# Transposes ahead of the value product in an attention and gated-convolution kernel

## The chip, the cores and the metric

The kernel runs on one core of one Trainium2 chip. The metric is the device time of one execution in microseconds (us); the figure for a kernel is the median of several executions. A core has five engines that run side by side, each with its own queue of instructions: TensorE (PE in the profile; its weight loads have a row of their own, PEld), VectorE (DVE), ScalarE (ACT), GpSimd (POOL) and SyncE (SP), which here only issues DMAs. TensorE writes its results to PSUM, a memory of eight banks, from which ScalarE or VectorE must copy them before the bank can be used again.

## The reference

Attention in which a query sees only the keys that fall into its own hash bucket, then a gated convolution and two products with weights. There are 4 batches, 8 heads, 768 positions and 64 numbers per head.

```python
q_bits = (np.einsum('bhsd,dk->bhsk', q, proj) > 0)      # 6 bits; k_bits alike
mask = q_bucket[:, :, :, None] == k_bucket[:, :, None, :]
scores = scale * np.matmul(q, k.transpose(0, 1, 3, 2))
scores = np.where(mask, scores, -1000000000.0)
attn = softmax(scores)
x = np.matmul(attn, v)              # heads side by side: 4 x 768 x 512
gate = sigmoid(causal depthwise convolution of x, 5 taps)
out = (gate * (x @ w_val)) @ w_out
```

## The kernel before, in words

A unit is one head of one batch (32 units), and a tile is 128 queries of a unit (6 per unit, 192 in all). The main loop goes over slots `k`, one per tile, and every engine but SyncE takes its instructions in the order in which the code issues them: the order in the loop's body is the order of the work. The tiles are in a pipeline, so that a slot works on several of them:

- `scores(k + 1)` (L236): TensorE makes the scores of 128 queries against 768 keys, in four products that add up two parts of the numbers, into one of two PSUM buffers `s`. The buffer comes free when `exponentials(k - 1)` has read it.
- `maxima(k)`, `factors(k)`, `shifts(k)` (L242, L248, L252): VectorE finds the rows' maxima and makes the factor `gs` and the shift `nb`.
- `exponentials(k)` (L260): ScalarE makes the exponentials `p` of a tile from `s`, `gs` and `nb`.
- `row_sums`, `recip` (L266, L270), once per two tiles: VectorE; `normalise(k - 2)` (L275): GpSimd multiplies `p` by the reciprocal.
- `transposes(k - 3)` (L284): TensorE transposes the six 128 x 128 blocks of `p`, three into each of two PSUM buffers `tp`. A `tp` buffer comes free when ScalarE has copied it.
- `keep_transposed(k - 4)` (L293), first in a slot: ScalarE copies the two `tp` into `pt`.
- `attn_v` (L307, L315): when the six tiles of a unit are in `pt`, TensorE multiplies them by the values into the PSUM buffer `av`, in six steps (`kb`). `step(avs)` is called twice in each odd slot, so that a unit's product takes three odd slots. Behind the last step, in the same call, ScalarE copies `av` to `x` in two instructions.

Into the same slots come steps of other work: `step(convs)` (the convolution, L327 to L342, mostly VectorE and GpSimd), `step(weights[...])` (the weights' split, in the first 60 slots), `step(moes)` (the two feed-forward products of an earlier batch, L369 and L394: four products of TensorE in a step, from slot 60 or so on, with some slots left out) and `step(preps)` (the next unit's operands: GpSimd's L166 and L169, DMAs, and once in four units `bits`, L197 and L200: TensorE multiplies four units by the hash planes, half in one slot and half in the next, and VectorE makes `u` of them. These products go into a `tp` buffer once a batch's feed-forward work exists, and into a PSUM buffer of their own before that).

Behind the loop stand the last unit's value product and the last batch's feed-forward work.

Of the kernel before, what the change touches and what calls it, by code (L numbers as in the profile page):

```python
# [26 lines left out]
def kernel(  # L27
# [18 lines left out]
    LAG = 3  # L46
# [71 lines left out]
    def load_conv():  # L118
        if conv_w.dtype == mybir.dt.int64:
            w = const.tile([P, NP * KW, 2], I32, name="cw64")  # L120
            nc.sync.dma_start(out=w, in_=conv_w.bitcast(I32).rearrange("p (n t) -> p n t", t=2))
            t = const.tile([P, NP * KW], FP32, name="cwt")
            yield
            a, d = yield from from_float64(w, t)
            yield
            nc.vector.tensor_tensor(out=cw_sb, in0=d, in1=a, op=ALU.add)
        else:
            nc.sync.dma_start(out=cw_sb, in_=conv_w)

    def load_weights(which):  # L130
        parts = [(src[:, c, :], hl[0][:, c, :], hl[1][:, c, :])
                 for src, hl in ((w_val, wv), (w_out, wo)) for c in range(NP)]
        for src, hi, lo in parts[which::2]:
            if src.dtype == mybir.dt.int64:
                w = wst.tile([P, 512, 2], I32, name="w64")
                nc.sync.dma_start(out=w, in_=src.bitcast(I32).rearrange("p (n t) -> p n t", t=2))
            else:
                w = wst.tile([P, 512], FP32, name="w32")
                nc.sync.dma_start(out=w, in_=src)
            yield  # L140
            yield from split_weight(w, hi, lo)

    def load_raw(i):
        if i < len(units):
            b, h = units[i]
            raws[i] = raw.tile([P, S], FP32, name="r")
            nc.sync.dma_start(out=raws[i], in_=qk[b, h])

    def load_values(i):
        b, h = units[i]  # L150
        if h % 2 == 0:
            vts[i] = vp.tile([P, KB, P], FP32, name="vt")
            nc.sync.dma_start(out=vts[i], in_=v[b, h // 2])
        else:
            vts[i] = vts[i - 1]

    def prep(i):

        if i >= len(units):
            return  # L160
        b, h = units[i]
        j = h % 4
        load_values(i)
        r = raws[i]
        aq, ak, bq, bk = stacks[i] = [stk.tile([P, S], FP32R, name=nm) for nm in ("aq", "ak", "bq", "bk")]
        nc.gpsimd.tensor_copy(out=aq, in_=r)  # L166
        if i > 1:
            yield
        nc.gpsimd.tensor_tensor(out=bq, in0=r, in1=aq.bitcast(FP32), op=ALU.subtract)  # L169
        nc.sync.dma_start(out=ak[0:D].bitcast(FP32), in_=aq[D:P].bitcast(FP32))  # L170
        nc.sync.dma_start(out=bk[0:D].bitcast(FP32), in_=aq[D:P].bitcast(FP32))
        nc.sync.dma_start(out=bk[D:P].bitcast(FP32), in_=bq[D:P].bitcast(FP32))
        nc.sync.dma_start(out=bq[D:P].bitcast(FP32), in_=aq[0:D].bitcast(FP32))
        if i == 1:
            yield
        u = cur["u"]
        nc.sync.dma_start(out=aq[D:M].bitcast(FP32), in_=u[32 * j:32 * j + 2 * NB].bitcast(FP32))
        nc.sync.dma_start(out=ak[D:M].bitcast(FP32), in_=u[32 * j + 2 * NB:32 * j + 4 * NB].bitcast(FP32))
        load_raw(i + 5)
        if j == 3 and i + 1 < len(units):  # L180
            yield
            yield from bits(i + 1)
# [21 lines left out]
    def first_bits():  # L204
        yield from bits(0)
        load_raw(5)

    def first_prep():

        r = raws[0]  # L210
        aq, ak, bq, bk = stacks[0] = [stk.tile([P, S], FP32R, name=nm) for nm in ("aq", "ak", "bq", "bk")]
        z = ps_t.tile([P, 512], FP32, name="tp")
        for g in range(4):
            nc.tensor.matmul(out=z[32 * g:32 * g + 2 * NB, 0:HS], lhsT=proj_sb[:, 2 * NB * (g // 2):2 * NB * (g // 2 + 1)],
                             rhs=r[:, HS * (g % 2):HS * (g % 2 + 1)], start=True, stop=True, tile_position=(0, 32 * g))
        nc.scalar.copy(out=aq[0:D], in_=r[0:D])
        nc.vector.tensor_copy(out=bk[D:P], in_=r[D:P])
        nc.vector.tensor_copy(out=ak[0:D], in_=r[D:P])
        nc.gpsimd.tensor_tensor(out=bk[0:D], in0=r[D:P], in1=bk[D:P].bitcast(FP32), op=ALU.subtract)
        for g in (0, 2, 3, 1):  # L220
            if g == 1:
                nc.vector.tensor_tensor(out=bq[D:P], in0=r[0:D], in1=aq[0:D].bitcast(FP32), op=ALU.subtract)  # L222
            nc.vector.tensor_scalar(out=(aq, ak)[g // 2][D:M, HS * (g % 2):HS * (g % 2 + 1)],
                                    in0=z[32 * g:32 * g + 2 * NB, 0:HS],
                                    scalar1=rows_sb[32 * g:32 * g + 2 * NB, 2:3],
                                    scalar2=rows_sb[32 * g:32 * g + 2 * NB, 3:4], op0=ALU.is_ge, op1=ALU.mult)
        nc.scalar.copy(out=bq[0:D], in_=r[0:D])

    def scores(k):
        i, qt = tiles[k]  # L230
        aq, ak, bq, bk = stacks[i]
        qs = slice(qt * P, (qt + 1) * P)
        s = ss[k] = ps_s.tile([P, 2, 512], FP32, name="s")
        for lq, rk, n in ((aq, ak, M), (bq, bk, P)):
            for hf in range(2):
                nc.tensor.matmul(out=s[:, hf, 0:HS], lhsT=lq[0:n, qs],  # L236
                                 rhs=rk[0:n, hf * HS:(hf + 1) * HS], start=n == M, stop=n == P)
# [35 lines left out]
    def normalise(k):  # L273
        p, _ = ps[k]
        nc.gpsimd.tensor_scalar(out=p, in0=p, scalar1=rcs.pop(k), scalar2=1.0, op0=ALU.mult, op1=ALU.mult)  # L275

    def transposes(k):
        p, _ = ps.pop(k)
        tps[k] = []
        for a in range(2):  # L280
            tp = ps_t.tile([P, 512], FP32, name="tp")
            for n in range(3):
                kb = 3 * a + n
                nc.tensor.transpose(out=tp[:, n * P:(n + 1) * P], in_=p[:, kb * P:(kb + 1) * P], identity=ident)  # L284
            tps[k].append(tp)
# [146 lines left out]
    def step(gens):  # L432

        while gens:
            try:
                return next(gens[0])
            except StopIteration:
                gens.pop(0)
# [6 lines left out]
    N = len(tiles)  # L445
    with tc.manual_schedule(engines=ENGINES):
        for i in range(5):
            load_raw(i)
        load_values(0)
        first_prep()  # L450
        weights = [[load_conv(), load_weights(0)], [load_weights(1)]]
        preps = [first_bits(), prep(1)]
        scores(0)
        next(preps[1])
        step(preps)
        step(weights[0])
        step(weights[1])
        turn = 0
        for k in range(N + LAG + 1):
            if 0 <= k - LAG - 1:  # L460
                keep_transposed(k - LAG - 1)
            pair = k % 2 == 0 and 0 <= k - 2 < N
            if k < N:
                maxima(k)
            if pair:
                row_sums(k - 2)
            if k < N:
                factors(k)
            if pair:
                recip(k - 2)  # L470
            if 0 <= k - 2 < N:
                normalise(k - 2)
            if k < N:
                shifts(k)
            if k + 1 < N:
                if tiles[k + 1][0] != tiles[k][0]:
                    finish(preps)
                    preps = [prep(tiles[k + 1][0] + 1)]
                scores(k + 1)
            if k < N:  # L480
                exponentials(k)
            if k >= 60 or k % 2:
                step(convs)
            for _ in range((1, 0, 2, 0, 2, 2)[k % 6]):
                step(weights[turn])
                turn = 1 - turn
            for _ in range(3 if cur["gates"] else 1):
                step(moes)
            cur["gates"] = max(0, cur["gates"] - 1)
            step(preps)  # L490
            if k % 2:
                step(avs)
                step(avs)
            if 0 <= k - LAG < N:
                transposes(k - LAG)
        accs[:] = [(ps_m, "m"), (ps_t, "tp"), (ps_s, "s"), (ps_t, "tp"), (ps_s, "s")]
        finish(avs)
        cur["gates"] = 0
        cur["end"] = True
        while convs:  # L500
            step(convs)
            step(moes)
        finish(moes)
# [59 lines left out]
```

## Time and profile before

| | |
|---|---|
| median of 3 executions | 626.68 us (626.09 to 627.2) |
| profiled execution, its own time | 627.79 us |
| its span, first to last instruction | 625.6 us |
| mean granted TensorE clock | 0.992 |
| TensorE, TensorE's weight loads busy | 588.2 us, 423.0 us |
| VectorE, ScalarE, GpSimd busy | 443.6, 421.3, 396.8 us |

How to read the rows: in a timeline a row has the start and the length in us, the engine, the line of the code, the operation, what it writes and reads, the shape, and how many instructions were merged (x8); in brackets stands how long the engine was idle before it and whose work ended that. A row of the waits has who waited for whom, the total in us, how often, and the longest. TensorE's products of full 32-bit numbers run in two passes, so four products of `attn_v` are eight records. The lengths of TensorE's records overlap: what a group costs is read from its start to the next group's start.

### The profile page before, as it was taken

To read this page: it belongs to the slowest core of one execution; us is meant where nothing else is said; L and a number is where in the kernel's file an instruction comes from. 1 tells how busy PE (TensorE), PEld (TensorE's weight loads), DVE (VectorE), ACT (ScalarE), POOL (GpSimd) and SP (SyncE) were. 2 spreads that over 40 slices of the span, in tenths; PEclk is the share of its full clock that TensorE was granted. 3 is DMA by queue.
4 is the path that set the end of the run, shared out by engine and by line. 5 is a ranking of instruction groups with operands and counts; after the bars stand their busy time and mean duration, and the time that the engine had idled before them with its cause. 6 is when DMAs were issued, how large, how long until landed. Compare 5 with 4: busy or idle time off the path is not lost.

```text
span 625.6 us, 10595 instructions
## 1 busy us (share of the span) xinstructions
PE 588.2 (94%) x3496; PEld 423.0 (68%) x3496; DVE 443.6 (71%) x1017; ACT 421.3 (67%) x881; POOL 396.8 (63%) x373
## 2 busy tenths in 40 slices
PE   5799888889999999999999999999999999999997
PEld 2656555556567777776667777676667777776895
DVE  5979897999876857477666867559575877665532
ACT  3777867677787766677796767667787767665400
POOL 3576978698956766566655768377563777544321
PEclk9799999999999999999999999999999999999999
DMA  6453625343523343224424233343423223300111
GB/s 226 129 156 76 176 70 168 77 122 82 132 72 87 81 124 71 72 81 114 107 78 123 68 79 92 77 113 79 124 56 76 53 46 91 77 18 1 50 51 50
DMA packets 23269, 56.76 MB, mean 91 GB/s; under 512 B 4296, under 2 KB 4296, under 8 KB 23216
## 3 DMA queue, kind: packets, MB, share of 16 engines
q1 hardware_dynamic: 23072, 56.06, 33.7%
q8 instruction: 28, 0.46, 0.3%
q14 instruction: 25, 0.20, 0.1%
q10 hardware_dynamic: 144, 0.03, 0.0%
HBM read 23.12 MB, written 6.29 MB: 47 GB/s over the span
## 4 chain that ended last, share of the span: by engine, by line
PE 66%; DVE 15%; ACT 12%; DMA 3%; issue 2%; POOL 1%; SPq 0%; ACTq 0%; DVEq 0%; POOLq 0%
PE av L307 17%; PE s L236 15%; PE tp L284 12%; PE m L394 8%; PE m L369 7%; ACT p L260 5%; DVE nm L242 5%; ACT pt L293 3%; DVE g L338 3%; ACT x L315 2%; PE tp L369 1%; PE tp L394 1%; PE s L394 1%; DVE u L200 1%; PE s L369 1%
## 5 line engine op out<-in xcount | busy, mean ns | idle before, releaser
L275 POOL TENSOR_SCALAR p<-p,ri 128x768 f32<-128x768 f32 x192 | 212.0, 1108 | 160.1 <-DVE nb L252 141.7
L242 DVE TENSOR_REDUCE nm<-s 128x1 f32<-128x768 f32 x192 | 182.5, 951 | 62.6 <-PE s L236 62.1
L293 ACT COPY pt<-tp 128x384 f32<-128x384 f32 x384 | 166.1, 485 | 85.0 <-PE tp L284 84.1
L260 ACT ACTIVATE p<-s,nb,gs 128x768 f32<-128x768 f32 x192 | 192.6, 1003 | 41.1 <-DVE nb L252 39.5
L284 PEld LDWEIGHTS tp<-ident,p 128*128 128x128 f32 x1152 | 130.1, 141 | 73.9 <-issue 44.7
L284 PE MATMUL tp<-ident,p 128*128 128x128 f32 x1152 | 164.9, 279 | 4.6 <-ACT pt L293 1.8
L307 PE MATMUL av<-pt,vt 128*64 128x384 f32 x768 | 146.2, 502 | 0.0
L236 PE MATMUL s<-ak,aq 76*128 76x384 f32 x384 | 117.8, 388 | 23.6 <-ACT p L260 21.2
L236 PE MATMUL s<-bk,bq 128*128 128x384 f32 x384 | 101.3, 345 | 0.4 <-DVE bq L222 0.4
L307 PEld LDWEIGHTS av<-pt,vt 128*64 128x64 f32 x768 | 47.3, 137 | 63.3 <-issue 62.7
L236 PEld LDWEIGHTS s<-ak,aq 76*128 76x128 f32 x384 | 59.0, 193 | 40.4 <-ACT p L260 36.6
L338 DVE SCALAR_TENSOR_TENSOR g<-x,cw_sb,g 128x768 f32<-128x768 f32 x64 | 83.2, 1300 | 2.2 <-POOL g L336 2.1
L236 PEld LDWEIGHTS s<-bk,bq 128*128 128x128 f32 x384 | 71.4, 193 | 0.8 <-issue 0.8
L380 POOL TENSOR_TENSOR hl<-ht,hh 128x384 fp32r<-128x384 f32 x32 | 32.3, 1009 | 43.7 <-DVE hh L378 43.7
L169 POOL TENSOR_TENSOR bq<-r,aq 128x768 fp32r<-128x768 f32 x31 | 59.1, 1908 | 0.1
L315 ACT COPY x<-av 64x384 f32<-64x384 f32 x64 | 30.4, 475 | 32.5 <-PE av L307 31.9
L252 DVE TENSOR_SCALAR nb<-nm,gs 128x1 f32<-128x1 f32 x192 | 40.5, 211 | 3.5
L369 PE MATMUL m<-xh,wv 128*128 128x384 f32 x200 | 42.7, 337 | 0.0
L374 DVE TENSOR_TENSOR ht<-m,g 128x384 f32<-128x384 f32 x25 | 13.9, 556 | 37.1 <-PE m L369 32.5
L328 POOL TENSOR_TENSOR xl<-x,xh 128x384 fp32r<-128x384 f32 x32 | 33.3, 1056 | 9.8 <-DVE xh L327 9.8
L260 ACT ACTIVATION_READ_ACCUMULATOR p<-s,nb,gs 128x1 f32 x192 | 39.1, 204 | 0.0
L394 PE MATMUL m<-wo,hh 128*128 128x512 f32 x144 | 38.2, 395 | 0.0
(84 smaller groups left out, 488.2 us busy)
## 6 DMA issues: line engine op xcount, KB each, us to landing
r<-in_qk_dram SPq DMA_DIRECT2D x32, 384.0 KB
vt<-in_v_dram SPq DMA_DIRECT2D x16, 384.0 KB
out_dram<-o SPq DMA_DIRECT2D x24, 256.0 KB
ak<-aq SPq DMA_DIRECT2D x31, 192.0 KB
bk<-aq SPq DMA_DIRECT2D x31, 192.0 KB
bk<-bq SPq DMA_DIRECT2D x31, 192.0 KB
bq<-aq SPq DMA_DIRECT2D x31, 192.0 KB
w<-in_w_val_dram SPq DMA_DIRECT2D x4, 512.0 KB
```

Of the source, the lines that this page charges most:

```text
L169: nc.gpsimd.tensor_tensor(out=bq, in0=r, in1=aq.bitcast(FP32), op=ALU.subtract)
L236: nc.tensor.matmul(out=s[:, hf, 0:HS], lhsT=lq[0:n, qs], rhs=rk[0:n, hf * HS:(hf + 1) * HS], start=n == M, stop=n == P)
L242: nc.vector.tensor_reduce(out=nm, in_=s[:, :, 0:HS], axis=AX.XY, op=ALU.max, negate=True)
L260: nc.scalar.activation(out=p, in_=s[:, :, 0:HS], func=AF.Exp, bias=nb, scale=gs.pop(k), accum_out=sm[:, k % 2, 0:1])
L275: nc.gpsimd.tensor_scalar(out=p, in0=p, scalar1=rcs.pop(k), scalar2=1.0, op0=ALU.mult, op1=ALU.mult)
L284: nc.tensor.transpose(out=tp[:, n * P:(n + 1) * P], in_=p[:, kb * P:(kb + 1) * P], identity=ident)
L293: nc.scalar.copy(out=pt[:, :, qo:qo + P], in_=tp[:, 0:HS].rearrange("p (a b) -> p a b", b=P))
L307: nc.tensor.matmul(out=av[s * D:(s + 1) * D, 0:HS], lhsT=vt[:, kb, hh * D:(hh + 1) * D], rhs=pt[kb // 3][:, kb % 3, :], start=(kb == 0), s ...
L315: nc.scalar.copy(out=x[hh * D:(hh + 1) * D, o:o + HS], in_=av[s * D:(s + 1) * D, 0:HS])
L338: nc.vector.scalar_tensor_tensor(out=g, in0=x[:, k:k + S], scalar=w, in1=g, op0=ALU.mult, op1=ALU.add)
L369: nc.tensor.matmul(out=acc[:, 0:HS], lhsT=wv[wi][:, c, j * P:(j + 1) * P], rhs=xs_[(c, o)][xi], start=(m == 0), stop=(m == 11))
L394: nc.tensor.matmul(out=acc, lhsT=hs[(o, j)][hi][:, tb * P:(tb + 1) * P], rhs=wo[wi][:, j, :], start=(m == 0), stop=(m == 11))
```

## The change

In a slot, `transposes(k - 3)` is issued ahead of the two `step(avs)` instead of behind them. Everything else stays. Even slots have no `step(avs)`, so that nothing moves in them.

```diff
             step(preps)
+            if 0 <= k - LAG < N:
+                transposes(k - LAG)
             if k % 2:
                 step(avs)
                 step(avs)
-            if 0 <= k - LAG < N:
-                transposes(k - LAG)
```

On TensorE, an odd slot and the even slot behind it, in a stretch without feed-forward products, before (`s` are scores, `av` the value product, `tp` the transposes):

```order
L236 MATMUL s<-ak,aq 128x384 x2
L236 MATMUL s<-bk,bq 128x384 x2
L307 MATMUL av<-pt,vt 64x384 x4
L284 MATMUL tp<-ident,p 128x128 x6
L236 MATMUL s<-ak,aq 128x384 x2
L236 MATMUL s<-bk,bq 128x384 x2
L284 MATMUL tp<-ident,p 128x128 x6
```

and after:

```order
L236 MATMUL s<-ak,aq 128x384 x2
L236 MATMUL s<-bk,bq 128x384 x2
L284 MATMUL tp<-ident,p 128x128 x6
L307 MATMUL av<-pt,vt 64x384 x4
L236 MATMUL s<-ak,aq 128x384 x2
L236 MATMUL s<-bk,bq 128x384 x2
L284 MATMUL tp<-ident,p 128x128 x6
```

The six transposes of the odd slot now stand next to its scores, and the value product next to the even slot's scores.

On ScalarE the order of the instructions is the same as before. At the end of a unit's value product, in the slot behind the odd one, one wait differs (`x` are the copies of the value product, `pt` those of the transposes, `p` the exponentials; the difference has before as - and after as +):

```order
 L315 COPY x<-av 64x384 [waits PE_49]
 L315 COPY x<-av 64x384
-L293 COPY pt<-tp 128x3x128 [waits PE_49] x2
+L293 COPY pt<-tp 128x3x128 x2
 L260 ACTIVATE p,sm<-s,nb,gs 128x768 [waits DVE_49,Pool_49]
```

The `pt` copies need no wait for TensorE of their own any more: the `x` copies ahead of them wait for an instruction of TensorE that now stands behind the transposes.

VectorE and GpSimd keep their order. SyncE's queue, which is not written out by hand, has three DMAs in another order at some places, as here (`vt` are values, `r` the queries and keys of a later unit, `bq` an operand of the next one):

```order
 L177 DMA aq<-u 12x768
-L153 DMA vt<-in_v_dram 128x768
-L173 DMA bq<-aq 64x768
-L147 DMA r<-in_qk_dram 128x768
+L147 DMA r<-in_qk_dram 128x768
+L153 DMA vt<-in_v_dram 128x768
+L173 DMA bq<-aq 64x768
```

The load of `r` moved ahead of the load of `vt` and of a copy within the core.

## The prediction

> **What bounds the kernel now.** First the page's engine shares, then the waits, then two stretches of the timeline.
>
> ```profile
> PE 588.2 (94%) x3496; PEld 423.0 (68%) x3496; DVE 443.6 (71%) x1017; ACT 421.3 (67%) x881; POOL 396.8 (63%) x373
> ```
>
> TensorE (PE) is busy nearly throughout. So only two things can move the time: the order's own cost on TensorE, and where TensorE waits. From the waits:
>
> ```profile
> ACT x L315 <- PE av L307: 31.9, 30, 3.8
> PEld s L236 <- ACT p L260: 36.6, 54, 2.6
> ```
>
> ScalarE (ACT) waits for the value product before it copies it out (us, times, longest); and 54 times the score product (S) waits for an exponential that must free its PSUM buffer. The timeline shows how these hang together, in a stretch without feed-forward products (start, length, engine). I write A for a slot's value products, T for its transposes; an odd slot is S, A, T, an even one S, T.
>
> ```profile
> 300.02 1.51 PE L307 MATMUL av<-pt,vt 128*64 128x384 f32 x8
> ...
> 301.57 0.97 ACT L315 COPY x<-av 64x384 f32<-64x384 f32 x2 [0.74 <-PE av L307]
> ...
> 302.57 0.86 ACT L293 COPY pt<-tp 128x384 f32<-128x384 f32 x2
> ...
> 303.32 1.01 ACT L260 ACTIVATE p<-s,nb,gs 128x768 f32<-128x768 f32 x1
> ...
> 304.47 0.62 PE L236 MATMUL s<-ak,aq 76*128 76x384 f32 x2 [0.43 <-ACT p L260]
> ...
> 305.38 1.51 PE L307 MATMUL av<-pt,vt 128*64 128x384 f32 x8
> ...
> 306.70 0.19 DVE L252 TENSOR_SCALAR nb<-nm,gs 128x1 f32<-128x1 f32 x1
> ...
> 306.98 0.91 POOL L275 TENSOR_SCALAR p<-p,ri 128x768 f32<-128x768 f32 x1 [1.34 <-DVE nb L252]
> 307.40 0.86 ACT L293 COPY pt<-tp 128x384 f32<-128x384 f32 x2 [1.25 <-PE tp L284]
> ...
> 307.45 0.59 PE L236 MATMUL s<-ak,aq 76*128 76x384 f32 x2
> ...
> 308.15 1.01 ACT L260 ACTIVATE p<-s,nb,gs 128x768 f32<-128x768 f32 x1
> 308.24 0.82 PE L284 MATMUL tp<-ident,p 128*128 128x128 f32 x6
> ...
> 309.30 0.62 PE L236 MATMUL s<-ak,aq 76*128 76x384 f32 x2 [0.24 <-ACT p L260]
> ...
> 314.13 0.62 PE L236 MATMUL s<-ak,aq 76*128 76x384 f32 x2 [0.25 <-ACT p L260]
> ```
>
> Two kinds of slot pairs (an odd slot and the even one behind it) are here. In the first, A is the last third of a head's value product: ScalarE copies x, then pt, then makes the exponential, and S starts. From A's start to that S it takes 304.47 - 300.02 = 4.45 us. I call these x pairs; there is one per head. In plain pairs x is absent; from 309.30 to 314.13 such a pair lasts 4.83 us, and the S behind its T (308.24 to 309.30, 1.06 us) still waits for an exponential. ScalarE does not overtake: nb was ready at 306.89 and ScalarE idle until 307.40, yet the exponential at 308.15 stayed behind the pt copies, which waited for T.
>
> With four feed-forward products in each slot:
>
> ```profile
> 501.35 1.51 PE L307 MATMUL av<-pt,vt 128*64 128x384 f32 x8
> 502.79 0.87 PE L284 MATMUL tp<-ident,p 128*128 128x128 f32 x6
> 503.42 0.59 PE L236 MATMUL s<-ak,aq 76*128 76x384 f32 x2
> ...
> 504.20 0.86 PE L369 MATMUL m<-xh,wv 128*128 128x384 f32 x4
> 504.90 0.82 PE L284 MATMUL tp<-ident,p 128*128 128x128 f32 x6
> 505.80 0.62 PE L236 MATMUL s<-ak,aq 76*128 76x384 f32 x2
> ...
> 506.60 0.86 PE L369 MATMUL m<-xh,wv 128*128 128x384 f32 x4
> 507.39 1.51 PE L307 MATMUL av<-pt,vt 128*64 128x384 f32 x8
> 508.83 0.88 PE L284 MATMUL tp<-ident,p 128*128 128x128 f32 x6
> ...
> 510.95 0.82 PE L284 MATMUL tp<-ident,p 128*128 128x128 f32 x6
> 511.52 0.60 PE L236 MATMUL s<-ak,aq 76*128 76x384 f32 x2
> ...
> 517.23 0.59 PE L236 MATMUL s<-ak,aq 76*128 76x384 f32 x2
> ```
>
> Here a plain pair (511.52 to 517.23, 5.71 us) has no wait: T to S takes 0.57. But the x pair that ends at 505.80 again took 505.80 - 501.35 = 4.45 us from A to S, though TensorE had another 0.8 us of products in it. The same number with and without feed-forward work says that in x pairs ScalarE's chain from the end of A decides, not TensorE.
>
> **The change, part by part.** No instruction is added or removed; in each of 96 odd slots six transposes go ahead of eight passes of value product.
>
> *x pairs.* The chain from A's start (A, x copies, pt copies, exponential, S) keeps its 4.45 us: the copies of T's result are behind the x copies on ScalarE, and those wait for A. But A now starts behind T. Before, S to A was 305.38 - 304.47 = 0.91 us, or 507.39 - 505.80 = 1.59 with feed-forward work. After, it is S to T (308.24 - 307.45 = 0.79, or 504.90 - 503.42 = 1.48) and T to A. The loop never has T in front of A; the tail has it once:
>
> ```profile
> 574.14 0.85 PE L284 MATMUL tp<-ident,p 128*128 128x128 f32 x6 [0.85 <-ACT pt L293]
> 574.92 4.40 PE L307 MATMUL av<-pt,vt 128*64 128x384 f32 x24
> ```
>
> That is 0.78 us, with T starting from a standstill, which costs S some 0.03 (0.62 against 0.59). The lower bound is T to S, 0.57, plus the 0.09 by which feed-forward to A (506.60 to 507.39, 0.79) exceeds feed-forward to T (504.20 to 504.90, 0.70): 0.66. I take 0.75, near the one row of the very pair. So A, and with it the pair's end, comes 0.79 + 0.75 - 0.91 = 0.63 us later, or 0.64. There are 32 heads; the last one's copies stand behind the loop, and in two the even slot has bit products and feed-forward products, and waits for VectorE's u instead:
>
> ```profile
> 253.93 0.55 PE L284 MATMUL tp<-ident,p 128*128 128x128 f32 x3 [0.38 <-DVE u L200]
> ```
>
> 29 x 0.635 = +18.4 us (bounds with 0.66 and 0.78: 16 to 19).
>
> *Plain pairs that TensorE fills.* After: S to T 1.48, T to A 0.75, A to S as A to T now (508.83 - 507.39 = 1.44) with 0.03 for the standstill, S to T 1.48, T to S 0.57: 5.75 against 5.71. No row has S behind A; the one border cost that I have, 0.09, either way gives 1.35 to 1.53 for A to S. I take +0.04 for 96 - 31 - 25 = 40 pairs: +1.6 (bounds -2 to +5).
>
> *Plain pairs that wait.* 54 waits less the 29 of x pairs leaves 25. T's copies could now run under A, so the exponential is early; the pair would be 0.79 + 0.75 + 1.47 + 0.79 + 0.57 = 4.37 against 4.83: -0.46 each, -11.5 in all. But most of these lie early, where VectorE (DVE) is nearly as full as TensorE, and the exponential also waits for nb:
>
> ```profile
> 42.70:183.00 140.30, 126.66 (x776) 81.35 (x776) 126.06 (x278) 107.12 (x233) 114.12 (x101) 0.99 0.41 110
> 183.00:571.00 388.00, 381.38 (x2318) 280.11 (x2318) 265.94 (x632) 279.86 (x584) 246.00 (x236) 1.00 0.32 81
> ```
>
> ```profile
> ACT p L260 <- DVE nb L252: 12.2, 15, 2.0
> ```
>
> (Columns: length, then PE, PEld, DVE, ACT, POOL busy; the wait is that of 40 to 183 us.) VectorE has 126.06 of 140.30 us. I take half: -5.8 (bounds 0 and -11.5).
>
> *Bit products.* Every fourth head TensorE makes bit products into T's PSUM buffers; A covers their evacuation by VectorE:
>
> ```profile
> 323.70 0.85 PE L197 MATMUL tp<-r,proj_sb 128*32 128x384 f32 x8
> ...
> 324.49 1.51 PE L307 MATMUL av<-pt,vt 128*64 128x384 f32 x8
> 324.62 0.68 DVE L200 TENSOR_SCALAR u<-tp,packed 128x384 fp32r<-128x384 f32 x1
> ```
>
> After, T starts at 324.49, its second half would at 324.8, but that buffer is free at 325.3: +0.5 in 4 slots (the other bit products of odd slots use another pool), +2.0 (bounds 0 to 3).
>
> *At nothing.* T needs POOL's normalised p: for T at 311.64 that was done at 307.89 (the POOL row at 306.98), so 1.4 us earlier is covered; without cover each T would wait. SP issues three loads per four or so heads in another order (r ahead of vt and bq); these are for later heads and nothing on TensorE waits for them now.
>
> Sum: 18.4 + 1.6 - 5.8 + 2.0 = +16.2. The profiled execution took 627.8 us (span 625.6), 1.1 above the median of 626.7; so 644 for it, 643 for the median.
>
> **Rivals.**
> 1. *Faster: no pause at the new neighbours.* If T to A cost 0.66 and A to S 1.35, an odd slot would save 0.09 twice against my sum: 96 x 0.18 = -17, so 626. It decides from 0.17 us a slot. Against it: the weight load of T behind A stands still until A has streamed:
>
> ```profile
> 311.64 0.64 PEld L284 LDWEIGHTS tp<-ident,p 128*128 128x128 f32 x6 [0.60 <-issue]
> ```
>
> The Trainium skill (TensorE: Matmul & The Clock Gate, Part 2: What happens when you issue a matmul) says that weight loads are pulled ahead of running matmuls when they go to the background buffer or to other row groups. By that rule S's weights would load under A and this rival's time would come. The trace does not agree at this border: the 0.60 us stand there.
> 2. *Faster: x pairs are no longer than now,* because the chain there is not what I think, and the plain waits go: 626.7 - 11.5 = 615. For it: T's result waits ready while A runs. Against it: the 4.45 twice, and ScalarE's order.
> 3. *Slower, but less:* every plain wait goes and the lower bounds hold: 16 - 2 - 11.5 + 2 = +4.5, so 631.
> 4. *Slower, more: T waits for POOL.* At 0.2 us in half of the slots, +10 on top, 653.
>
> ```profile
> PEld tp L284 <- POOL p L275: 10.6, 16, 1.2
> ```
>
> Only 16 such waits exist, and the room above speaks against it.
> 5. *The order does not matter:* gains and x pairs cancel, 627.
>
> **How the numbers follow.** My forecast (636 to 650) has 0.66, rival 3 (630 to 636) 0.16, rival 4 0.09, rival 1 0.05, rival 2 0.03, rival 5 0.01. Rivals 1 and 5 give 0.03 for within 0.2% (what a measurement here can tell from no change); faster has 0.06, slower 0.91. The range 632 to 650 leaves out rivals 1, 2, 5, most of 4 and a little of 3.
>
> **What would show it.** In the profile after: A to the next S in x pairs still 4.45, with A 0.63 later in its slot, ScalarE idle before x copies for longer than 31.9 us in total, and S waiting for the exponential longer in x pairs, less elsewhere. T to A 0.75, A to S near 1.47. I am wrong if x pairs last as before, or if T waits for POOL or for pt copies in ordinary odd slots.

## The result, and the profile after

The changed kernel took 647.29 us (median; 646.69 to 648.09) against 626.94 us of the kernel before, run beside it: a ratio of 1.0312, 95% interval 1.0297 to 1.0327. The forecast of 643 with its range of 632 to 650 holds it. The profiled execution took 647.13 us (span 645.0); the prediction's sum for it was 644.

The page's engine shares of after, busy us and instructions, answer to the first line that the prediction shows:

```profile
PE 598.5 (93%) x3496; PEld 432.5 (67%) x3496; DVE 442.2 (69%) x1017; ACT 422.0 (65%) x881; POOL 393.8 (61%) x373
```

TensorE has the same 3496 matmuls, with 10.3 us more of busy time in a span that is 19.4 us longer; its share hardly moved, so this line does not tell where the time went. The waits of after tell more (us in total, times, longest):

```profile
ACT x L315 <- PE av L307: 50.6, 32, 3.8
PEld s L236 <- ACT p L260: 37.7, 47, 2.4
PEld tp L284 <- POOL p L275: 5.4, 7, 1.0
```

The first was 31.9 us in 30 waits: ScalarE now stands 18.7 us longer before the x copies. The second hardly moved in total (36.6 before), though it has 7 waits fewer. The third halved (10.6 before): T waits for POOL less than it did, not more.

The timeline of after, TensorE alone, where feed-forward products fill the slots (start, length):

```profile
515.70 0.60 PE L236 MATMUL s<-ak,aq 76*128 76x384 f32 x2
...
517.18 0.82 PE L284 MATMUL tp<-ident,p 128*128 128x128 f32 x6
517.93 1.51 PE L307 MATMUL av<-pt,vt 128*64 128x384 f32 x8
519.37 0.62 PE L236 MATMUL s<-ak,aq 76*128 76x384 f32 x2
...
522.36 0.62 PE L236 MATMUL s<-ak,aq 76*128 76x384 f32 x2 [0.44 <-ACT p L260]
...
528.12 0.60 PE L236 MATMUL s<-ak,aq 76*128 76x384 f32 x2
...
533.87 0.59 PE L236 MATMUL s<-ak,aq 76*128 76x384 f32 x2
```

The x pair from 515.70 to 522.36 takes 6.66 us; before, such pairs took 6.04. From A (517.93) to its last S it is 4.43 (4.45 before); what has grown is the way to A. T to A is 0.75, A to the next S 1.44. The plain pair from 528.12 to 533.87 takes 5.75 (5.71 before).

And without feed-forward products, TensorE and ScalarE of after:

```profile
302.08 0.59 PE L236 MATMUL s<-ak,aq 76*128 76x384 f32 x2
...
306.44 0.59 PE L236 MATMUL s<-ak,aq 76*128 76x384 f32 x2
...
307.22 0.82 PE L284 MATMUL tp<-ident,p 128*128 128x128 f32 x6
...
307.97 1.51 PE L307 MATMUL av<-pt,vt 128*64 128x384 f32 x8
...
309.53 0.97 ACT L315 COPY x<-av 64x384 f32<-64x384 f32 x2 [0.89 <-PE av L307]
...
310.52 0.87 ACT L293 COPY pt<-tp 128x384 f32<-128x384 f32 x2
...
311.27 1.01 ACT L260 ACTIVATE p<-s,nb,gs 128x768 f32<-128x768 f32 x1
...
312.42 0.61 PE L236 MATMUL s<-ak,aq 76*128 76x384 f32 x2 [0.43 <-ACT p L260]
```

T (307.22, 0.82 long) is through at 308.04. Its copies start at 310.52: ScalarE has the x copies ahead of them, which wait for A until 309.53. That is 2.5 us in which a finished result lies. A to S is 4.45 again, and the x pair 5.98 instead of 5.35. The plain pair before it (302.08 to 306.44) takes 4.36 instead of 4.81: there the waits went.

From the starts of the same score products in both timelines the span's difference comes apart so (us; positions in before):

| stretch | difference | made of |
|---|---|---|
| start to 42.70 | +1.66 | all before the first steady pair |
| 42.70 to 183.06 | +2.31 | nine x pairs +6.50, the other pairs -4.20 |
| 183.06 to 559.79 | +14.76 | x pairs +12.35, four odd slots with bit products +2.93, 29 filled pairs +1.26, waiting pairs -1.78 |
| the rest | +0.61 | the last x pair and the tail |

### The profile page after: what moved, and what is told of

Its sections match the earlier page's. It is cut to its first block, busy times and chain, and to the rows that moved or that the text cites. A ratio compares the mean times of both kernels' runs of the same rounds, so it can differ in the third digit from the quotient of the medians.

```text
span 645.0 us, 10624 instructions
## 1 busy us (share of the span) xinstructions
PE 598.5 (93%) x3496; PEld 432.5 (67%) x3496; DVE 442.2 (69%) x1017; ACT 422.0 (65%) x881; POOL 393.8 (61%) x373
## 4 chain that ended last, share of the span: by engine, by line
PE 68%; DVE 15%; ACT 13%; issue 4%; DMA 1%; POOL 0%; ACTq 0%; POOLq 0%; DVEq 0%
PE av L307 18%; PE s L236 18%; PE tp L284 12%; PE m L394 7%; PE m L369 6%; ACT p L260 6%; DVE nm L242 5%; ACT pt L293 3%; ACT x L315 2%; DVE g L338 2%; DVE u L200 1%; PE tp L369 1%; PE tp L394 1%; PE s L394 1%; DVE o L93 1%
## 5 line engine op out<-in xcount | busy, mean ns | idle before, releaser
L275 POOL TENSOR_SCALAR p<-p,ri 128x768 f32<-128x768 f32 x192 | 209.2, 1093 | 171.8 <-DVE nb L252 153.2
L284 PEld LDWEIGHTS tp<-ident,p 128*128 128x128 f32 x1152 | 136.4, 143 | 39.6 <-issue 14.9
L236 PE MATMUL s<-ak,aq 76*128 76x384 f32 x384 | 120.1, 394 | 24.9 <-ACT p L260 23.0
L338 DVE SCALAR_TENSOR_TENSOR g<-x,cw_sb,g 128x768 f32<-128x768 f32 x64 | 81.1, 1267 | 2.2 <-POOL g L336 2.1
```

The lines of the kernel that those rows point to most:

```text
L236: nc.tensor.matmul(out=s[:, hf, 0:HS], lhsT=lq[0:n, qs], rhs=rk[0:n, hf * HS:(hf + 1) * HS], start=n == M, stop=n == P)
L338: nc.vector.scalar_tensor_tensor(out=g, in0=x[:, k:k + S], scalar=w, in1=g, op0=ALU.mult, op1=ALU.add)
```

## The experiments

The theory: the loss sits in the x pairs, since ScalarE's queue has the x copies, which wait for A, ahead of the pt copies and the exponential. Rivals: the new neighbours T, A and S cost TensorE time in every odd slot; or the early transposes disturb something else.

**Ahead, but not in x slots; ahead in x slots alone.** The two halves of the change:

```diff
-            if 0 <= k - LAG < N:
+            ahead = k % 6 != 1        # the second kernel: k % 6 == 1
+            if ahead and 0 <= k - LAG < N:
                 transposes(k - LAG)
             if k % 2:
                 step(avs)
                 step(avs)
+            if not ahead and 0 <= k - LAG < N:
+                transposes(k - LAG)
```

> T ahead of A in all odd slots except those where a head's value product ends (one in three), which keep T behind A. Theory: the loss of x pairs (18.8 us in the trace) is gone, and what is left is the plain pairs' gain of 5.3 against 1.3 for the filled plain pairs, 2.9 for the slots with bit products and about 1 at the start: 627 us (624 to 630), no change. Rival A (the loss is spread over all odd slots, 20.4 / 96 = 0.21 us each): 627 + 64 x 0.21 = 640.

> T ahead of A only in the odd slots where a head's value product ends (32 of 96). Theory: the whole loss of x pairs and none of the rest: 627 + 19 = 646 us (642 to 649), with every x pair 0.63 us longer than before. Rival A: 627 + 32 x 0.21 = 634.

Measured: 630.07 us for the first (ratio 1.0034, 1.0017 to 1.0051) and 646.58 for the second (1.0286, 1.0262 to 1.0309), beside 628.32 for the kernel before. So one odd slot in three carries nearly the whole loss. The timeline of the second kernel, TensorE alone:

```profile
516.55 0.59 PE L236 MATMUL s<-ak,aq 76*128 76x384 f32 x2
...
518.77 1.51 PE L307 MATMUL av<-pt,vt 128*64 128x384 f32 x8
...
523.20 0.62 PE L236 MATMUL s<-ak,aq 76*128 76x384 f32 x2 [0.44 <-ACT p L260]
```

The x pair takes 6.65 us, A to S 4.43. Over 17 undisturbed x pairs after 183 us it has +11.01 (0.65 each; after has +10.97). Its bit slots and 28 of its 29 filled pairs stand within 0.03 of before, each; one of the waiting pairs is 1.60 longer. In the first kernel the same 17 x pairs have -0.02; the filled pairs have +1.26 and the bit slots +2.95, as in after.

The first kernel missed its 627, by 3. From 42.70 to 183.06 us its pairs other than x pairs gain 0.19 us, where in after they gain 4.20 (and 3.37 in a kernel of a later experiment that has after's order in this stretch). What is late next there is VectorE. The wait of the exponential for nb in this stretch, before, after, and in the first kernel:

```profile
ACT p L260 <- DVE nb L252: 11.8, 14, 2.0
```

```profile
ACT p L260 <- DVE nb L252: 21.5, 27, 2.2
```

```profile
ACT p L260 <- DVE nb L252: 26.4, 31, 2.2
```

VectorE is busy for 126 of the 140 us there. Where x pairs stay short it has little slack, and what the order saves in waiting pairs comes back as waits for the maxima; in after it catches up during the longer x pairs. That the second follows from the first is read from these sums, not tested alone. In these traces, of one execution each, the two halves do not add up to the whole in this stretch. By the medians no such thing shows: alone the first half costs 1.8 us and the second 18.3, together 20.1 beside the 20.4 of the whole change.

**The x copies twice.** If the chain behind A decides, lengthening it must show in full:

```diff
-        for s in range(2):
+        for s in (0, 1, 0, 1):
             o = KW - 1 + s * HS
             nc.scalar.copy(out=x[hh * D:(hh + 1) * D, o:o + HS], in_=av[s * D:(s + 1) * D, 0:HS])
```

> The changed kernel with each x copy made twice (the result stays the same). Theory: the x copies are serial on the chain that ends an x pair, so A to the next S takes 4.45 + 0.97 = 5.42 us in every x pair, and the time is 647 + 31 x 0.97 = 677 us (672 to 680). If they lay beside other work: less than 655.

One execution: 686.94 us. Its timeline, TensorE and ScalarE:

```profile
369.50 1.51 PE L307 MATMUL av<-pt,vt 128*64 128x384 f32 x8
...
371.06 1.96 ACT L315 COPY x<-av 64x384 f32<-64x384 f32 x4 [1.99 <-PE av L307]
...
374.94 0.62 PE L236 MATMUL s<-ak,aq 76*128 76x384 f32 x2 [0.43 <-ACT p L260]
```

A to S is 5.44 for 4.45: the 0.99 of the added copies comes out whole, although TensorE has feed-forward products in these slots. The 17 undisturbed x pairs after 183 us are 0.99 longer each than in after. The total is 10 us above the forecast. Part of that lies in plain pairs behind x pairs, in stretches without feed-forward products (two of them after 183 us are 1.60 and 3.06 longer), and VectorE waits longer for x there; its wait in after and in this kernel:

```profile
DVE xh L327 <- ACT x L315: 18.0, 12, 7.0
```

```profile
DVE xh L327 <- ACT x L315: 32.7, 12, 10.6
```

This is one execution, and at a lower granted clock (0.967 over the run, 0.90 from 100 to 183 us), so how much of the rest each makes is open.

**The x copies behind the pt copies.** The theory's remedy: the x copies of a head are kept, and issued in the even slot behind the exponential. This is done to after and, apart, to before.

```diff
...
+        def keep():
+            for s in range(2):
+                o = KW - 1 + s * HS
+                nc.scalar.copy(out=x[...], in_=av[...])
+            if hh == 1:
...
+                convs.append(pair_x(b, c, x, cur["g"], cur["xs"]))
+        keeps.append(keep)
...
+            if k % 2 == 0:
+                while keeps:
+                    keeps.pop(0)()
```

> The changed kernel, but ScalarE's x copies are issued one slot later, behind that slot's pt copies and exponential. Theory (in x pairs the chain A, x copies, pt copies, exponential, S sets the end, and T ahead of A pushes that chain back by 0.63 us): the chain no longer holds x or A, so x pairs fall to what plain pairs take: with feed-forward products 5.76 instead of 6.67 us, without them about 4.4 to 4.9 instead of 5.98. Some 29 us less than the changed kernel: 618 us (612 to 624), below the kernel before. Rival A (the new neighbours on TensorE, T to A and A to S, cost about 0.2 us in each odd slot): the time stays near 647.

> The kernel before (T behind A) with the same move of the x copies. Theory: x pairs lose their 0.3 (with feed-forward) to 0.5 us of wait and become plain pairs, 5.72 and 4.83 us: about 11 us less than before, 616 us (612 to 620). Rival A says nothing of it. If the x copies' place did not matter, 627.

Measured: 631.57 us (ratio 1.0064, 1.0040 to 1.0088) on after and 638.32 (1.0155, 1.0140 to 1.0170) on before. With T ahead the loss shrinks from 20.4 us to 3.3, but both kernels miss what was expected, by 13.6 and 22.3 us. Of the two, T ahead is now the faster, by 6.8 us. In the first the x pairs are 26.7 us shorter in sum than in after, near the 29 expected, and the waits of ScalarE's x copies for A are all but gone. TensorE's timeline shows one of 5.75 us (336.25 to 342.00), as long as a plain one, with no wait in it. But only six of the x pairs with feed-forward products come to 5.75 to 5.78. Five stay at 5.97 to 6.00, such as the one from 353.81 to 359.78, where ScalarE stands 1.96 us for nb, that is for VectorE:

```profile
ACT x L317 <- PE av L307: 4.7, 2, 3.8
```

```profile
336.25 0.60 PE L236 MATMUL s<-ak,aq 76*128 76x384 f32 x2
...
342.00 0.59 PE L236 MATMUL s<-ak,aq 76*128 76x384 f32 x2
...
358.64 0.99 ACT L260 ACTIVATE p<-s,nb,gs 128x768 f32<-128x768 f32 x1 [1.96 <-DVE nb L252]
...
359.78 0.61 PE L236 MATMUL s<-ak,aq 76*128 76x384 f32 x2
```

The other pairs take 12.4 us of the first kernel's gain back. What the expectation overlooked is who reads x: VectorE casts it to xh in the same slot, and its queue keeps order too. Its wait for x, in before (in after it is 18.0 us), in the first kernel and in the second:

```profile
DVE xh L327 <- ACT x L315: 10.0, 6, 6.3
```

```profile
DVE xh L330 <- ACT x L317: 25.2, 12, 5.9
```

```profile
DVE xh L330 <- ACT x L317: 36.4, 12, 6.4
```

The second kernel's timeline, all engines, shows what stands behind such a wait:

```profile
346.56 0.97 ACT L317 COPY x<-av 64x384 f32<-64x384 f32 x2
...
346.78 0.59 PE L236 MATMUL s<-ak,aq 76*128 76x384 f32 x2
...
347.06 1.67 DVE L330 CAST xh<-x 128x384 fp32r<-128x384 f32 x2 [2.44 <-ACT x L317]
...
348.92 0.94 DVE L242 TENSOR_REDUCE nm<-s 128x1 f32<-128x768 f32 x1
...
350.40 0.99 ACT L260 ACTIVATE p<-s,nb,gs 128x768 f32<-128x768 f32 x1 [1.99 <-DVE nb L252]
...
351.53 0.62 PE L236 MATMUL s<-ak,aq 76*128 76x384 f32 x2 [0.86 <-ACT p L260]
```

VectorE stood 2.44 us for x with the next maxima queued behind; the exponential and S follow late, and the slot takes 4.75 us. So part of the stall had moved from ScalarE's queue to VectorE's.

**The casts a slot later as well.** If that reading holds, the convolution step with the casts must go behind the late copies' slot:

```diff
+            if k >= 60 or k % 2:
+                step(convs)
             if k % 2 == 0:
                 while keeps:
                     keeps.pop(0)()
...
-            if k >= 60 or k % 2:
-                step(convs)
```

> As e1, and VectorE's casts of x are issued one slot later than there, so that they no longer stand ahead of the next maxima while x is late. Theory (what e1 lost against its forecast is VectorE held up by casts that wait for x): the slots behind x pairs lose their extra 0.3 to 1.2 us, some 5 us less than e1: 626 us (623 to 629). Rival B (ScalarE itself has no room for the x copies there): no change from e1, 631.

> As e2 (T behind A, x copies behind pt copies), with the casts one slot later. Theory: the slots behind x pairs, which had 0.3 to 1.6 us more than before in e2, come back to their length before, 11 us less than e2: 627 us (623 to 630). Rival B: 638 as e2.

Measured: 623.36 us with T ahead (ratio 0.9936, 0.9913 to 0.9958) and 622.77 with T behind (0.9917, 0.9894 to 0.9941), beside 627.98. The first lies in its range and the second 0.2 us below its own. VectorE's wait for x in the second falls to one, and the same slot, which took 4.75 us, takes 3.66 (340.02 to 343.68), the maxima ahead of the cast:

```profile
DVE xh L330 <- ACT x L317: 4.1, 1, 4.1
```

```profile
340.02 0.60 PE L236 MATMUL s<-ak,aq 76*128 76x384 f32 x2
...
340.12 0.95 DVE L242 TENSOR_REDUCE nm<-s 128x1 f32<-128x768 f32 x1
...
341.43 0.62 DVE L330 CAST xh<-x 128x384 fp32r<-128x384 f32 x2
...
343.68 0.59 PE L236 MATMUL s<-ak,aq 76*128 76x384 f32 x2
```

Both are faster than the kernel before. With x out of the chain the two orders of T and A differ by 0.6 us, inside the intervals: the 20 us that the change costs show only with the x copies ahead of the pt copies. Neither kernel comes down to the 618 and 616 us that were expected of the moved copies alone; what holds the last 5 to 7 us was not followed up. (The later casts move some feed-forward steps by a slot, so these kernels' slots do not match those of before one to one.)

**The order kept where bit products stand.** After, with T behind A in slots that have bit products in T's buffers (the flag `bits` is set where they are issued):

```diff
+            ahead = not cur["bits"]
+            cur["bits"] = False
-            if 0 <= k - LAG < N:
+            if ahead and 0 <= k - LAG < N:
                 transposes(k - LAG)
...
+            if not ahead and 0 <= k - LAG < N:
+                transposes(k - LAG)
```

> The changed kernel, with T behind A in those odd slots alone where the bit products lie in T's own PSUM buffers (4 of 96). Theory: A again covers VectorE's evacuation there, each of the four slots loses its 0.74 us, and nothing else moves: 647.3 - 3.0 = 644.3 us (643 to 645.5). If the bit products had no part in the loss: 647.

Measured: 643.73 us (1.0245, 1.0218 to 1.0273), beside 628.02. The four slots are back to their length of before, 0.00. After's timeline shows what they cost:

```profile
331.93 0.85 PE L197 MATMUL tp<-r,proj_sb 128*32 128x384 f32 x8
...
332.71 0.55 PE L284 MATMUL tp<-ident,p 128*128 128x128 f32 x3
333.58 0.55 PE L284 MATMUL tp<-ident,p 128*128 128x128 f32 x3 [0.33 <-DVE u L200]
...
334.06 1.51 PE L307 MATMUL av<-pt,vt 128*64 128x384 f32 x8
335.50 0.62 PE L236 MATMUL s<-ak,aq 76*128 76x384 f32 x2
```

T's second half starts 0.87 us after its first, and A only behind it.

**T ahead where nothing fills the slot.** The best parts together: x copies and casts later, T ahead only in odd slots without feed-forward products and without bit products in T's buffers (the flag `busy` is set where either is issued; the excerpt has neither those lines nor the later copies and casts).

```diff
+            ahead = not cur["busy"]
+            cur["busy"] = False
-            if 0 <= k - LAG < N:
+            if ahead and 0 <= k - LAG < N:
                 transposes(k - LAG)
...
+            if not ahead and 0 <= k - LAG < N:
+                transposes(k - LAG)
```

> As e5, with T ahead of A only in odd slots in which TensorE has neither feed-forward products nor bit products on T's buffers; elsewhere T stays behind A. Theory: it keeps the gain of the waiting pairs (0.46 us each), and drops the 0.04 of the filled pairs and the 0.74 of four slots with bit products, some 4 us less than e5: 622 us (619 to 626), below the kernel before.

Measured: 621.76 us (0.9909, 0.9886 to 0.9933). It is the lowest median of all and below both kernels, but its interval does not part it from the 622.77 of T always behind. The two differ in the order of the free odd slots alone, so that with short x pairs the gain of the waiting pairs is 1.0 us by the medians, and not clear of the noise.

## Why the prediction was right, point by point

The mechanism and the path were right, and the sum of +16.2 us stands against +19.34 in the two traces. Of the 3.1 us between them 1.7 lie in the start, 1.1 in the x pairs with the tail, 0.9 in the bit products; the two other terms are 0.5 too high.

- **x pairs.** Forecast 29 x 0.635 = +18.4 us. Measured: +0.62 to +0.67 in the undisturbed ones, +6.50 in the first stretch (one of its nine pairs has 0.18 and one 1.79), +12.35 in the second, and 0.61 at the end with the tail: 18.9 to 19.5. The two pairs that the forecast left out, which wait for VectorE's u, have 0.06 and 0.04. A to S stayed at 4.43 to 4.45 in the undisturbed pairs, T to A came out at the 0.75 taken. That this is ScalarE's order and not TensorE's neighbours is shown three ways: the half of the change in x slots carries the loss alone, a longer x copy lengthens the pair by as much, and with x copies and casts later the two orders take the same time. The page Perfetto Trace Analysis of the Trainium skill (Tensor Engine Instruction (MATMUL, LD_WEIGHTS)) says that VectorE and ScalarE work strictly in order; the 2.5 us that T's result lies ready in after, and the 2.44 us for which VectorE waits for x with the maxima behind, agree.
- **Filled pairs.** Forecast +0.04 each, measured +0.04 (5.75 for 5.71) in 29 pairs, +1.26 in place of +1.6.
- **Waiting pairs.** One came out at 4.36 where 4.37 was worked out. But the pair that the forecast timed (309.30 to 314.13, 4.83) takes 4.92 in after (316.79 to 321.71): the pt copies no longer hold its exponential, and it waits for nb, since VectorE does a step of the convolution ahead of the maxima:

```profile
317.73 1.44 DVE L338 SCALAR_TENSOR_TENSOR g<-x,cw_sb,g 128x768 f32<-128x768 f32 x1
...
320.57 0.99 ACT L260 ACTIVATE p<-s,nb,gs 128x768 f32<-128x768 f32 x1 [0.81 <-DVE nb L252]
```

  The total, -4.20 - 1.78 = -6.0, meets the -5.8, which was half of the bound. The halving was a guess at VectorE's limit, and that it came out so near is luck. The traces show the limit, and that it goes with the x pairs: where these stay short, the early gain is 0.19 us and not 4.20. In that one trace, -5.8 would have been wrong as a price of this term by itself.
- **Bit products.** Mis-sized: forecast +0.5 a slot, +2.0; measured 0.73, +2.93. The term counted the wait for the buffer and left out the border: in this slot bits to T take 0.78 as bits to A did (0.79), T to A 0.48 behind its second half, and A to S 1.44, so the order alone adds 0.12 (0.78 + 0.75 + 1.44 against 2.85 from the bit products to S with T behind), and the wait was 0.60 instead of 0.5.
- **Start.** Forecast nothing, measured +1.66 us. Most of this is not the order's. At the score product that starts at 32.15 in before, TensorE has done the same work in the same order in both kernels, and after is already 1.02 us later. Its granted clock was down to half there, in a stretch in which TensorE had no pause: first after, then before (columns: length, busy time of PE, PEld, DVE, ACT, POOL, then the clock, 0.50 and 1.00, DMA share, GB/s).

```profile
31.00:37.00 6.00, 6.00 (x24) 5.01 (x25) 3.19 (x11) 4.58 (x10) 2.73 (x3) 0.50 0.76 219
```

```profile
31.00:37.00 6.00, 5.64 (x38) 3.90 (x36) 3.91 (x10) 4.77 (x11) 4.37 (x5) 1.00 0.77 209
```

  The score product at 30.59 in after takes 1.01 us, the same one in before 0.62. The first half of the change and the kernel with the bits' order kept have after's order up to 42.70, keep a clock of 1.00 in that window, and are 1.09 and 0.48 us late at 32.15 and 0.82 and 0.59 at 42.70. The second half, which has before's order up to 42.70, is 0.26 earlier. So with the same order on TensorE the start differs by up to 1.1 us between executions. What lowers the clock is not shown.
- **At nothing.** T waits for POOL for 5.4 us in 7 waits (10.6 in 16 before), so rival 4 does not show. SP's other order of loads does not show either: TensorE's waits for DMAs are 0.2 us in after and 0.5 in before.
- **The rivals.** Rival 2 (x pairs no longer) falls with the 0.65; rivals 3 and 5 with the size. Rival 1 falls because A to S takes 1.44, as A to T did, and T to A 0.75. Its -17 was also too much by the forecast's own chain: in the 31 x pairs a shorter A to S is worth nothing, so that 96 x 0.09 + 65 x 0.09 = 14.5 us would have been its gain. The weights of S behind A stand until A has streamed:

```profile
335.50 0.30 PEld L236 LDWEIGHTS s<-ak,aq 76*128 76x128 f32 x2 [0.60 <-ACT pt L293]
```

  The 0.60 is the same as at T's loads behind A before. The Trainium skill (TensorEngine Tiling (Array Packing), Key Properties) says that a change of tiling mode drains TensorE. A's form here is 128 by 64 and its neighbours' are not, and 0.60 us of standing loads agree with it (behind the bit products, 128 by 32, the next load stands for 0.62 us); the rule that rival 1 rested on does not show at this border. No run here changes the form alone, so it is not shown that the form is the cause.

## What to carry to other kernels

Before moving work on one engine, read on the engine that evacuates it which instruction stands ahead in its queue and what that one waits for: a result that is ready 1.5 us earlier is worth nothing behind a copy that waits for the work just moved back. To shorten such a chain, move the late copy behind the urgent ones, and then its readers too, since each of their engines keeps order as well. A gain in waits has to be checked against the engine that is next to full, because it can come back there as another wait.

## What the runs showed of the hardware that was not expected

The granted clock of one core can fall to half for some six microseconds while TensorE is busy without a pause (0.50 from 31 to 37 us in after), and in other executions of the same instructions it stays at 1.00 there. And the value product costs the same border whichever neighbour follows: A to T took 1.44 before, A to S 1.44 after, with the next weight load standing for 0.60 us in both.
